# A decode layer on one core: QK in four column groups, one exp per half of K, P permuted by matmuls, PV on 128 columns, shared weights

## Chip, cores, metric

One core of a Trainium2 chip. Its engines are called PE (matmuls), DVE (vector work), ACT (activations, here also copies) and SP (which issues the loads) below; SBUF is the memory that loads land in, PSUM the one that matmuls write to. The metric is the device time of one execution in microseconds (us). The kernel before takes 381.83 us (median of 3 runs, 381.77 to 382.25).

## The reference, cut to what matters

One decode step of a transformer layer: attention over a window of cached keys and values, then a gated MLP, for a batch of 4, one token each.

```python
# B=4, D=576, Hq=32 query heads, Hkv=16, window 4096 of 16384 keys, Dh=128, F=4608, bf16
q = layernorm(x) @ wq                                   # 576 x 4096
k, v = k_cache[:, :, -4096:], v_cache[:, :, -4096:]      # 4 x 16 x 4096 x 128 each
p = softmax(q . k * Dh**-0.5);  o = p . v               # two query heads per kv head
h = x + o @ wo                                          # 4096 x 576
h2 = h + (relu(layernorm(h) @ W_gate) * (layernorm(h) @ W_up)) @ W_down
```

K and V are 67.1 MB each and all the weights 25.4 MB: 159.6 MB have to come in for one input and one output of 4.6 KB each. This is a kernel of loads.

## The kernel before

K and V come in 16 groups each (group `g` is four kv heads of batch `g // 4`, one load of 4.19 MB), into a ring of four slots in SBUF. K's loads run four groups ahead of V's: K4, V0, K5, V1 and so on. One DMA queue issues all loads, in order, and each waits until the last reader of its slot is done. That wait ties the loads to the engines.

```python
def place(name, off, size, reader, make, key=None):       # a load waits for the last reader of its bytes
    for blk in range(off // 64, (off + size) // 64):
        r = owner.get(blk)
        if r is not None and r not in deps: deps.append(r)
        owner[blk] = reader
    P.dma("sync", ("L",) + name, make, semk, deps)
...
place((kind, g), off, TILE, ("QK", g, 1) if kind == "K" else ("PV", g), ...)
```

K has to be turned (DVE transposes 32x32 blocks, in two halves `w` of 128x4096 each), multiplied with q on PE, and after a batch's four groups the softmax follows. PV of group `g - 4` follows QK of group `g` on PE. Its result in PSUM holds more than is wanted, so DVE selects (`select_o`: multiply by a mask, add up).

```python
def pe_qk(g, w, heads=range(4)):
    for a in heads:
        for cb in range(4):
            first = a == cb == 0
            if first:
                deps.append(("TRA", g, w))                # each half of QK waits for its own half of the turn
            ...
            pe(("QK", g, w), lambda e, ...: e.matmul(
                bank[SB[b % 2] + w], lhsT=arena[:, wo_:wo_ + 128],   # 128 columns, mostly zeros (masked q)
                rhs=bass.AP(tensor=arena, offset=off, ap=[[AW, 128], [128, 64]] + steps), ...), deps)

def pe_pv(g):                                             # four column groups of 32, one bank, two banks in turn
    o_ps = bank[OB[g % 2]]
    ...  # PV(g) waits for: L V g, P of this batch, the selection of g - 2
            pe(("PV", g), lambda e, j=j, tq=tq, k=k: e.matmul(
                o_ps[32 * j:32 * j + 32, :], lhsT=pT[:, qd * 1024 + tq * 32:][:, 0:32], rhs=v[:, tq * 512:(tq + 1) * 512], ...), deps)

def do_k(g):                                              # order in the program; each engine runs its part in order
    turn_k(g, 0)
    ...
    flush()                                               # the selection of the PV of the turn before, put off until here
    turn_k(g, 1)
    ...
    pe_qk(g, 0)
    pe_qk(g, 1)
    ...                                                   # then PV(g - 4)
```

## Time and profile before

| | before |
|---|---|
| time, median | 381.83 us |
| span of the profiled run | 379.9 us |
| main load queue | 159.59 MB, 98.0% of 16 engines' span |
| PE / DVE / ACT busy | 74% / 59% / 10% |
| last landing of W_down, then to the end | 376.4 us, 3.5 us |

From the page: busy time of each engine, then the share of the DMA engines and the GB/s in 40 equal slices of the span (a 9 is 90% or more), then the queues with packets, MB and share of 16 engines' span. q1 carries the loads, q8 fetches instructions.

```profile
span 379.9 us, 3671 instructions
...
PE 279.6 (74%) x1629; PEld 93.6 (25%) x1629; DVE 223.1 (59%) x157; ACT 37.6 (10%) x95; POOL 16.5 (4%) x40
...
DMA  8999999999999999999999999999999999999993
GB/s 332 442 414 412 442 442 438 431 400 440 442 440 428 422 421 437 442 431 430 417 435 438 436 417 435 423 438 442 438 412 431 431 436 435 430 433 428 421 405 159
...
q1 hardware_dynamic: 6500, 159.59, 98.0%
q8 instruction: 12, 0.20, 0.2%
```

The DMA row never falls below 9 between its two ends: the loads are the bound. In the packet records a 32 KB packet takes 1.213 us on each of 16 engines, which is 432 GB/s. One batch of K and V (eight loads, 33.6 MB) therefore takes 77.6 us, and a pair of K and V 19.4 us.

The groups that matter, with line, engine, operation, shapes, count, busy time, mean ns of one, and idle time of the engine before them: QK (L453), K's turn (L435) and PV (L500).

```profile
L453 PE MATMUL psb<-sb_arena 128*128 128x512 bf16 x512 | 209.2, 579 | 10.5 <-DVE sb_arena L435 8.0
L435 DVE STREAM_TRANSPOSE sb_arena<-sb_arena 128x4096 f32<-128x4096 f32 x32 | 156.0, 4898 | 47.6 <-DMA sb_arena<-in_A_k_cache_dram 47.6
...
L500 PE MATMUL psb<-sb_arena,sb_pp 128*32 128x512 bf16 x512 | 35.8, 431 | 13.3 <-DMA sb_arena<-in_A_v_cache_dram 6.7
```

From the view of waits (who waited for whom, us in total, times, longest): DVE waits for K's landing, and PE hardly waits for the turn on DVE.

```profile
DVE sb_arena L435 <- DMA sb_arena<-in_A_k_cache_dram: 47.6, 11, 8.4
...
PE psb L453 <- DVE sb_arena L435: 8.0, 3, 3.4
```

And DVE's timeline around one group (start, duration, instruction, and in brackets the idle time before it with what ended it):

```profile
200.64 4.45 DVE L435 STREAM_TRANSPOSE sb_arena<-sb_arena 128x4096 f32<-128x4096 f32 x1 [8.36 <-DMA sb_arena<-in_A_k_cache_dram]
205.01 0.65 DVE L508 TENSOR_TENSOR sb_o_tmp<-psb,sb_qm 128x512 f32<-128x512 f32 x1
205.70 1.04 DVE L512 TENSOR_REDUCE sb_o_sel<-sb_o_tmp 128x128 f32<-128x512 f32 x1
206.66 4.44 DVE L435 STREAM_TRANSPOSE sb_arena<-sb_arena 128x4096 f32<-128x4096 f32 x1
```

### The profile page before, as it was taken

Reading aid. Unit: us, or ns where it says so; the run is one execution under the profiler, and the core shown is the slowest. Engines: PE = TensorE matmul, PEld = TensorE weight load, DVE = VectorE, ACT = ScalarE, POOL = GpSimd, SP = SyncE. Lnnn points to the kernel's source line nnn. Section 1 sums busy time; section 2 is a strip of 40 time slices with the busy share of each in tenths; the row PEclk is TensorE's granted clock in tenths of the full one; section 3 lists DMA queues with packets and bytes.
Section 4 is the critical chain, followed back from the end, with each engine's and each line's share of the span. In section 5 each row is a group of like instructions: output and inputs, shape, how many; then the busy total and the mean of one; then the engine's idle time right before and its main releaser. Section 6 shows DMA issues by size and latency. Waiting matters only on the chain.

```text
span 379.9 us, 3671 instructions
## 1 busy us (share of the span) xinstructions
PE 279.6 (74%) x1629; PEld 93.6 (25%) x1629; DVE 223.1 (59%) x157; ACT 37.6 (10%) x95; POOL 16.5 (4%) x40
## 2 busy tenths in 40 slices
PE   0047999998959992979996939799969537335445
PEld 0022323322222221222222213222212213124224
DVE  0796799979385917875828279756464455012011
ACT  1112000016000007000000050000000340000100
POOL 8800000000000000000000000000000000000000
PEclk9996999999979996798997888989989956756667
DMA  8999999999999999999999999999999999999993
GB/s 332 442 414 412 442 442 438 431 400 440 442 440 428 422 421 437 442 431 430 417 435 438 436 417 435 423 438 442 438 412 431 431 436 435 430 433 428 421 405 159
DMA packets 6522, 159.81 MB, mean 421 GB/s; under 512 B 744, under 2 KB 876, under 8 KB 1516
## 3 DMA queue, kind: packets, MB, share of 16 engines
q1 hardware_dynamic: 6500, 159.59, 98.0%
q8 instruction: 12, 0.20, 0.2%
q14 instruction: 2, 0.02, 0.0%
q10 hardware_dynamic: 8, 0.00, 0.0%
HBM read 159.58 MB, written 0.00 MB: 420 GB/s over the span
## 4 chain that ended last, share of the span: by engine, by line
PE 44%; DMA 37%; DVE 14%; POOL 2%; issue 1%; ACT 0%; SPq 0%; POOLq 0%
PE psb L453 38%; DMA sb_arena<-in_A_k_cache_dram 18%; DMA sb_arena<-in_B_W_down_dram 11%; DVE sb_arena L435 11%; DMA sb_arena<-in_A_v_cache_dram 8%; PE psb L500 4%; POOL sb_arena L303 2%; DVE sb_o_sel L512 1%; DVE sb_o_tmp L508 1%; PE psb L537 0%; ACT sb_arena L421 0%; SPq L286 0%; PE psb L525 0%; PE psb L520 0%; PE psb L472 0%
## 5 line engine op out<-in xcount | busy, mean ns | idle before, releaser
L453 PE MATMUL psb<-sb_arena 128*128 128x512 bf16 x512 | 209.2, 579 | 10.5 <-DVE sb_arena L435 8.0
L435 DVE STREAM_TRANSPOSE sb_arena<-sb_arena 128x4096 f32<-128x4096 f32 x32 | 156.0, 4898 | 47.6 <-DMA sb_arena<-in_A_k_cache_dram 47.6
L453 PEld LDWEIGHTS psb<-sb_arena 128*128 128x128 bf16 x512 | 56.7, 113 | 153.8 <-issue 130.2
L478 ACT ACTIVATE sb_pp<-psb,sb_stat 128x512 bf16<-128x512 f32 x32 | 24.9, 840 | 246.8 <-DVE sb_stat L473 246.8
L500 PE MATMUL psb<-sb_arena,sb_pp 128*32 128x512 bf16 x512 | 35.8, 431 | 13.3 <-DMA sb_arena<-in_A_v_cache_dram 6.7
L500 PEld LDWEIGHTS psb<-sb_arena,sb_pp 128*32 128x32 bf16 x512 | 13.5, 106 | 38.2 <-issue 22.5
L508 DVE TENSOR_TENSOR sb_o_tmp<-psb,sb_qm 128x512 f32<-128x512 f32 x16 | 10.8, 678 | 18.1 <-PE psb L500 18.1
L460 DVE TENSOR_REDUCE sb_stat<-psb 128x1 f32<-128x1024 f32 x4 | 4.8, 1208 | 24.1 <-PE psb L453 24.1
L487 DVE STREAM_TRANSPOSE sb_pp<-sb_pp 128x2048 bf16<-128x2048 bf16 x8 | 18.0, 2277 | 1.4 <-ACT sb_pp L478 1.4
L671 PE MATMUL psb<-sb_arena,sb_hnT 128*32 128x384 bf16 x120 | 9.1, 480 | 11.3 <-DMA sb_arena<-in_B_W_up_dram 8.4
L512 DVE TENSOR_REDUCE sb_o_sel<-sb_o_tmp 128x128 f32<-128x512 f32 x16 | 16.6, 1038 | 0.5
L537 PE MATMUL psb<-sb_o_sel,sb_selw 128*32 128x32 f32 x128 | 2.4, 232 | 16.3 <-DVE sb_o_sel L512 16.3
L678 DVE TENSOR_TENSOR sb_pp<-psb,sb_pp 128x384 bf16<-128x384 f32 x3 | 1.5, 550 | 18.5 <-PE psb L671 18.5
L378 PE MATMUL psb<-sb_ident_b,sb_xn_bf 4*128 4x4 bf16 x4 | 0.3, 174 | 13.7 <-DVE sb_xnd_bf L367 13.7
L391 PE MATMUL psb<-sb_arena,sb_xnT 128*32 128x512 bf16 x32 | 3.6, 631 | 8.9 <-DMA sb_arena<-in_A_wq_dram 8.9
L520 PE MATMUL psb<-sb_stat,sb_sameh 128*128 128x1 f32 x8 | 1.9, 311 | 9.1 <-DVE sb_stat L518 9.1
L671 PEld LDWEIGHTS psb<-sb_arena,sb_hnT 128*32 128x32 bf16 x120 | 4.1, 133 | 15.7 <-DMA sb_arena<-in_B_W_up_dram 8.8
L625 PE MATMUL psb<-sb_arena,sb_oT 128*32 128x288 bf16 x64 | 4.0, 445 | 4.9 <-DMA sb_arena<-in_A_wo_dram 4.9
L303 POOL MEMSET sb_arena<- 128x8192 f32 x1 | 6.9, 6925 | 0.0
L478 ACT ACTIVATION_READ_ACCUMULATOR sb_pp<-psb,sb_stat 128x1 f32 x32 | 6.4, 200 | 0.0
L537 PEld LDWEIGHTS psb<-sb_o_sel,sb_selw 128*32 128x32 f32 x128 | 1.9, 143 | 17.5 <-DVE sb_o_sel L512 17.5
L704 PE MATMUL psb<-sb_arena,sb_pp 128*32 128x144 bf16 x144 | 4.6, 301 | 1.7 <-DMA sb_arena<-in_B_W_down_dram 0.7
(125 smaller groups left out, 73.3 us busy)
## 6 DMA issues: line engine op xcount, KB each, us to landing
sb_arena<-in_A_k_cache_dram SPq DMA_DIRECT2D x16, 4096.0 KB, 17.6
sb_arena<-in_A_v_cache_dram SPq DMA_DIRECT2D x16, 4096.0 KB, 24.3
sb_arena<-in_A_wo_dram SPq DMA_DIRECT2D x1, 4608.0 KB, 26.8
sb_arena<-in_B_W_gate_dram SPq DMA_DIRECT2D x1, 4608.0 KB, 32.0
sb_arena<-in_B_W_up_dram SPq DMA_DIRECT2D x1, 4608.0 KB, 42.2
sb_arena<-in_A_wq_dram SPq DMA_DIRECT2D x1, 4096.0 KB, 21.6
sb_arena<-in_B_W_down_dram SPq DMA_DIRECT2D x3, 1296.0 KB, 40.9
sb_arena<-in_B_W_down_dram SPq DMA_DIRECT2D x1, 864.0 KB, 42.4
```

Of the source, the lines that this page charges most:

```text
L303: pool("c_qW", lambda e: e.memset(arena[:, 0:2 * QWW].bitcast(FP32), 0.0))
L435: dve(("TRA", g, w), lambda e: e.transpose(out=dst, in_=src), [("L", "K", g)] if w == 0 else [])
L453: pe(("QK", g, w), lambda e, off=off, steps=steps, wo_=wo_, qd=qd, first=first, last=a == cb == 3: e.matmul(bank[SB[b % 2] + w], lhsT=aren ...
L460: dve(("MAX", b), lambda e: e.tensor_reduce(out=stat[:, b, 0:1], in_=s_ps, axis=AX.X, op=ALU.max, negate=True), [("QK", 4 * b + 3, 1)])
L478: act(("EXP", b, w), lambda e, w=w, a=a: e.activation(out=bass.AP(tensor=pp, offset=4096 + a // 2 * 2048 + w * 1024 + a % 2, ap=[[8192, 12 ...
L487: dve(("PTR", b, w), lambda e: e.transpose(out=dst, in_=src), [("EXP", b, w), ("PV", 4 * b - 1) if b else "QMM"])
L500: pe(("PV", g), lambda e, j=j, tq=tq, k=k: e.matmul(o_ps[32 * j:32 * j + 32, :], lhsT=pT[:, qd * 1024 + tq * 32:][:, 0:32], rhs=v[:, tq * ...
L508: dve(("OS", g), lambda e: e.tensor_tensor(out=o_tmp[:, :].rearrange("p (t d) -> p t d", t=4), in0=o_ps.rearrange("p (t d) -> p t d", t=4) ...
L512: dve(("OSEL", g), lambda e: e.tensor_reduce(out=o_sel[:, qd, :], in_=o_tmp[:, :].rearrange("p (t d) -> p d t", t=4), axis=AX.X, op=ALU.ad ...
L537: pe(("OT", b), lambda e, q=q, qd=qd: e.matmul(ot_ps[32 * qd:32 * qd + 32, 0:32], lhsT=selw[:, qd, 32 * q:32 * q + 32], rhs=o_sel[:, qd, 3 ...
L671: pe(("GU", g, c // 4), lambda e, g=g, m=m, j=j, lo=lo, c=c: e.matmul(bank[3 * g + m][32 * j:32 * j + 32, 0:384], lhsT=hnT[:, c if c < 4 e ...
L704: pe("DOWN", lambda e, j=j, r=r, n=n, wv=wv: e.matmul(bank[0][32 * n:32 * n + 32, 0:144], lhsT=hhT[:, r * 128 + 32 * j:r * 128 + 32 * j + 32],
```

## The change

Its intent is to take work off PE and ACT. QK no longer multiplies by a 128-column matrix that is mostly zeros; each of four heads has its own group of 32 columns, and the four run side by side. The scores then stand by head, one exp per half does (8 instead of 32). P stands in other rows than V wants, so 64 small matmuls permute it and 32 masked copies spread it. PV now multiplies 128 columns at once into four banks. Matmuls that follow each other with the same weights load them once (`mm_same`). The up-projection weights come in two pieces, and DOWN uses two column groups of 288 instead of four of 144.

```diff
+def mm_same(e, out, lhsT, rhs, start, stop, tile, pos):      # a matmul that keeps the weights of the one before
+    return e.add_instruction(mybir.InstMatmult(... ldweights=False, ...))
...
-        def pe_qk(g, w, heads=range(4)):
+        def pe_qk(g):
+            for cb in range(4):
+                for w in range(2):
+                    for a in range(4):
+                        if cb == w == a == 0:
+                            deps = [("TRA", g, 1)]
+                            if qd == 0 and b:
+                                deps += [("EXP", b - 1, 1), ("MAX", b - 1), ("EV", b - 1, 1)]
+                        lhsT = arena[:, b * 2048 + cb * 512 + g % 4 * 128 + a * 32:][:, 0:32]
+                        out_ = bank[w][32 * a:32 * a + 32, :]
+                        # w == 1: mm_same(...), else e.matmul(...)
...
+        def remap(b):                                        # P to V's rows, then spread under a mask
+            for n in range(4):
+                for i in range(4):
+                    pe(("RM", b, n // 2), ... lhsT=to_v[:, n, :], ...)
+            for h in range(2):
+                for a in range(4):
+                    deps = [("RM", b, h), ("PV", 4 * b - 1) if b else "QMM"] if a == 0 else []
+                    if h: dve(("EV", b, 1), ... e.tensor_scalar(out=out_, in0=src, scalar1=m4[:, a:a + 1], ...), deps)
+                    else: act(("EV", b, 0), ... e.activation(out=out_, in_=src, func=ACT.Copy, scale=m4[:, a:a + 1]), deps)
...
         def pe_pv(g):
-                        deps = [("L", "V", g), ("PTR", b, 0), ("PTR", b, 1), ("OS", g - 2) if g >= 2 else "xT"]
+                        deps = [("L", "V", g), ("EV", b, 0), ("EV", b, 1)] + ([("OSD", g - 1), ("OSC", g - 1)] if g else [])
+                    lhsT = pT[:, qd * 1024 + k * 128:][:, 0:128]
+                    # into bank[2 + j]; j > 0: mm_same(...)
...
         for g in range(NTILE):
+            turn_k(g, 0)
+            if g == 4: soft(0); remap(0)
+            flush()                                          # the selection
+            turn_k(g, 1)
+            pe_qk(g)
+            if g % 4 == 3 and g > 3: soft(g // 4)
+            if g >= 4: do_v(g - 4)
+            if g % 4 == 3 and g > 3: remap(g // 4)
```

Because the two halves of QK share weights, `w` moved inside the loop over `cb`, and QK now waits for the second half of the turn.

## The prediction

> **What bounds the kernel now: the load queue.** The page's queue line gives 159.59 MB on the main queue, 98.0% of 16 engines' span; the slice row for DMA reads 9 from slice 2 to 39. In the trace's packet records a 32 KB packet takes 1.213 us on each of 16 engines, 432 GB/s, nearly everywhere. The Trainium skill ("DMA: Bandwidth & Descriptors", Specifications) gives a fabric ceiling of 435 GB/s; this trace agrees. 159.6 MB at 432 GB/s is 369 us. The rest of the 379.9 us span: loads start moving at 2.2 to 3.0 us; most engines finish at 373, but three only at 376.05; last landing 376.4; then 3.5 us of tail (last W_down matmuls, copy, store). The late engines: twelve 16 KB instruction fetches share these engines, and each delays its engine by about 1.5 us; an engine with two is 3 us late, and the last landing waits for the latest.
>
> PE (74% busy), DVE (59%), ACT (10%) are not the bound. The chain of waits shows "PE 44%", but through slot releases, while the queue is practically never empty.
>
> **What the change does.**
> - Bytes loaded: unchanged. Order: wq before the first K; the up-projection weights in two pieces.
> - QK: 512 matmuls of 128 columns at 441 ns become 512 in four column groups. Estimate 3.5 us per K group instead of 14.1, if four strided streams run side by side as PV's four contiguous ones did (1.84 us per 32).
> - PV: from 1.84 us per group to 32 full-width matmuls; estimate 4 x 1.84 = 7.4 us (twice that at a 0.5 clock).
> - Sum per group 11 us instead of 16, against 19.4 us of loading per K+V pair. PE busy falls from 280 to about 200 us.
> - Softmax: 32 exps (840 ns each) become 8; P's transposes shrink from 18 us to about 5; new are 64 small permutation matmuls and 32 masked copies (0.4 to 0.6 us each). V's selection costs DVE about 1 us more per group. The slow K transposes (first pair 14.3 us against 8.9) go, saving 13 us. DVE about 215 us, ACT about 40.
> - 768 of 1454 matmuls load no weights: about 9 instruction fetches instead of 12.
> - The tail: up's last part leaves 1 us of gate/up work after landing instead of 4. DOWN uses two column groups of 288 instead of four of 144, so up to twice as slow (240 ns per step at clock 0.5), but starts about 3 us earlier.
>
> **On the critical path:** almost nothing. The queue keeps its bytes and rate; slots come free sooner (before, the load issued at 41.1 us came as the queue ran dry near 43 us, costing about 0.4 us; that goes). Fewer fetches take perhaps 0 to 1.5 us off the last landing, by chance of where they fall. The tail may change by a few tenths.
>
> **Predicted: 380.8 us, 379.0 to 382.6 us.** Chances: faster by over 2% 0.02, within 2% 0.95, slower 0.03.
>
> **Signs of being right:** DMA still 97 to 98% of the span; last W_down landing 374.5 to 376.5 us; PE busy near 200 us, idle before PV; ACT and DVE little changed; longer queue waits for slots that never empty the queue.
>
> **What would make it wrong:** strided streams not running side by side, or a PE clock mostly at 0.5, so that QK+PV pass 19.4 us per pair and starve the queue (slower); a gap in the loads where the new softmax chain holds up PV 12 to 15, and with it wo's load; DOWN falling behind the last landing (1 to 3 us slower); or a load rate above 432 GB/s, which nothing here suggests.

## More of the kernel before

DVE waited 8.36 us for K to land, turned its first half, made the selection of the last PV (L508, L512), and turned the second half. The chain of waits has PE starting QK of the first half at 205.14 us, while DVE is still selecting: PE and DVE overlap here.

## The result, and the profile after

403.07 us (median of 4, 402.58 to 405.1) against 382.04 us for the kernel before. A ratio here is the mean time of one kernel's fast runs over that of the other's of the same rounds, so not quite the ratio of the medians: 1.056, 95% interval 1.053 to 1.060. The change is slower, by well over the range that was predicted.

| | before | after |
|---|---|---|
| span | 379.9 us | 403.2 us |
| PE / DVE / ACT busy | 279.6 / 223.1 / 37.6 us | 216.4 / 228.0 / 54.2 us |
| main queue, share of the span | 98.0% | 93.0% |
| one batch of loads, V6's issue to V10's | 77.8 us | 86.3 us |
| last landing of W_down | 376.4 us | 394.7 us |
| from it to the end | 3.5 us | 8.5 us |
| end of the last PV | 332.0 us | 371.1 us |

("One batch" is the time between the issue of V's loads 6 and 10 on the load queue: 167.14 and 244.89 us before, 181.00 and 267.34 us after.) The profiled run after was the slowest of its four (405.1 us), so these figures are 2 us on the high side of the median. Of the 23.3 us between the spans, 18.3 are a later last landing and 5.0 a longer end. In the packet records each DMA engine is idle for 17.6 us on average between its first packet and the last few microseconds, against 0.9 us before. That is nearly all of the later landing.

The page after:

```profile
span 403.2 us, 2703 instructions
...
PE 216.4 (54%) x1495; PEld 40.9 (10%) x727; DVE 228.0 (57%) x202; ACT 54.2 (13%) x89; POOL 16.2 (4%) x39
...
DMA  9999999999999999769999999399999997999990
GB/s 361 419 416 462 418 419 452 429 419 434 440 423 423 452 421 419 325 260 416 410 427 424 436 423 436 128 419 413 423 423 436 434 429 328 395 417 411 418 403 10
...
q1 hardware_dynamic: 6632, 159.59, 93.0%
q8 instruction: 9, 0.15, 0.1%
```

The same 159.59 MB come in, but the GB/s row has holes: 325 and 260, 128, and 328 near the end. Two stretches of the span, with busy time and instructions of each engine, granted clock, DMA share and GB/s, show the first hole:

```profile
160.00:170.00 10.00, 0.06 (x4) 0.06 (x4) 9.92 (x7) 0.00 (x0) 0.00 (x0) 0.52 0.88 380
170.00:180.00 10.00, 10.00 (x61) 1.36 (x24) 4.26 (x2) 0.00 (x0) 0.00 (x0) 0.80 0.53 210
```

From 160 to 170 us PE did nothing and DVE was busy throughout; from 170 to 180 us PE was busy throughout and DVE less than half. Neither is the bound over the whole, yet each waits for the other. The load queue in that stretch (the start of an issue):

```profile
173.90 0.53 SPq L247 DMA_DIRECT2D sb_arena<-in_A_k_cache_dram  x1
181.00 0.54 SPq L247 DMA_DIRECT2D sb_arena<-in_A_v_cache_dram  x1
```

The load issued at 173.90 us waited for QK to finish with its slot, and the queue had nothing else to do: from 169.90 to 174.20 us the view of windows shows a DMA share of 0.00.

The groups: the turn, QK (L466 with L34 for the matmuls that share weights) and PV (L530 with L34).

```profile
L442 DVE STREAM_TRANSPOSE sb_arena<-sb_arena 128x4096 f32<-128x4096 f32 x32 | 141.0, 4430 | 12.2 <-DMA sb_arena<-in_A_k_cache_dram 12.2
L466 PE MATMUL psb<-sb_arena 128*32 128x512 bf16 x256 | 42.2, 628 | 137.4 <-DVE sb_arena L442 137.4
L34 PE MATMUL psb<-sb_arena,sb_pp 128*128 128x512 bf16 x384 | 108.9, 394 | 0.0
L530 PE MATMUL psb<-sb_arena,sb_pp 128*128 128x512 bf16 x128 | 50.9, 398 | 9.3 <-DVE sb_o_tmp L543 9.3
...
L34 PE MATMUL psb<-sb_arena 128*32 128x512 bf16 x256 | 44.1, 652 | 0.0
```

QK's four strided streams do run side by side: 32 matmuls take 3.9 us, PV's 32 take 7.0 us. The estimates were 3.5 and 7.4. The waits:

```profile
PE psb L466 <- DVE sb_arena L442: 137.4, 16, 14.6
...
DVE sb_arena L442 <- DMA sb_arena<-in_A_k_cache_dram: 12.2, 8, 2.4
```

PE now waits 137 us for K's turn, where it waited 8. And DVE waits 12 us for K to land instead of 48: K is there, DVE is late. (L34 is the line of the helper `mm_same`, so QK and PV share it and are told apart by shapes.) DVE's timeline around one ordinary group:

```profile
201.26 1.38 DVE L543 TENSOR_TENSOR sb_o_tmp<-psb,sb_fm 32x512 f32<-32x512 f32 x2 [7.00 <-PE psb L34]
202.67 0.69 DVE L546 TENSOR_TENSOR sb_o_tmp<-sb_o_tmp,sb_fm 64x512 f32<-64x512 f32 x1
203.39 1.02 DVE L547 TENSOR_REDUCE sb_o_sel<-sb_o_tmp 128x128 f32<-128x512 f32 x1
204.33 8.76 DVE L442 STREAM_TRANSPOSE sb_arena<-sb_arena 128x4096 f32<-128x4096 f32 x2
219.66 1.38 DVE L543 TENSOR_TENSOR sb_o_tmp<-psb,sb_fm 32x512 f32<-32x512 f32 x2 [6.57 <-PE psb L34]
```

From one selection (201.26) to the next (219.66) are 18.4 us, and they are a ring: selection 3.1 us, second half of the next K's turn 4.4 us, QK 3.9 us (to 212.65, by the load queue's issue), PV 7.0 us, selection. Each waits for the one before. DVE sits idle for 6.57 us of it, PE for 7.5. And at the end of a batch:

```profile
146.73 1.38 DVE L491 STREAM_TRANSPOSE sb_pp<-sb_pp 128x512 bf16<-128x512 bf16 x2 [0.84 <-ACT sb_pp L487]
155.42 2.73 DVE L508 TENSOR_SCALAR sb_pp<-psb,sb_m 128x512 bf16<-128x512 f32 x4 [7.31 <-PE psb L497]
158.07 4.43 DVE L442 STREAM_TRANSPOSE sb_arena<-sb_arena 128x4096 f32<-128x4096 f32 x1
162.43 1.34 DVE L543 TENSOR_TENSOR sb_o_tmp<-psb,sb_fm 32x512 f32<-32x512 f32 x2
...
165.45 8.76 DVE L442 STREAM_TRANSPOSE sb_arena<-sb_arena 128x4096 f32<-128x4096 f32 x2
```

DVE waits 7.31 us for the permutation, which stands behind a PV on PE, before it makes its half of the masked copies (L508). The next K's turn stands behind those copies in DVE's order, and its second half behind another selection: it is done at 169.9 us, about 23 us after the softmax's transposes of P began (146.73).

### The profile page after: what moved, and what is told of

It reads as the page before. It is cut to its first block, busy times and chain, and to the rows that moved or that the text cites. A ratio compares the mean times of both kernels' runs of the same rounds, so it can differ in the third digit from the quotient of the medians.

```text
span 403.2 us, 2703 instructions
## 1 busy us (share of the span) xinstructions
PE 216.4 (54%) x1495; PEld 40.9 (10%) x727; DVE 228.0 (57%) x202; ACT 54.2 (13%) x89; POOL 16.2 (4%) x39
## 3 DMA queue, kind: packets, MB, share of 16 engines
q1 hardware_dynamic: 6632, 159.59, 93.0%
## 4 chain that ended last, share of the span: by engine, by line
PE 50%; DVE 36%; DMA 12%; issue 1%; ACT 0%; SPq 0%; DVEq 0%
PE psb L34 29%; DVE sb_arena L442 18%; DMA sb_arena<-in_A_k_cache_dram 12%; PE psb L530 8%; PE psb L466 6%; DVE sb_o_tmp L543 5%; DVE sb_o_sel L547 3%; DVE sb_pp L508 3%; DVE sb_o_tmp L546 2%; DVE sb_stat L471 1%; PE psb L726 1%; PE psb L497 1%; PE psb L646 1%; PE psb L688 1%; PE psb L638 0%
## 5 line engine op out<-in xcount | busy, mean ns | idle before, releaser
L442 DVE STREAM_TRANSPOSE sb_arena<-sb_arena 128x4096 f32<-128x4096 f32 x32 | 141.0, 4430 | 12.2 <-DMA sb_arena<-in_A_k_cache_dram 12.2
L466 PE MATMUL psb<-sb_arena 128*32 128x512 bf16 x256 | 42.2, 628 | 137.4 <-DVE sb_arena L442 137.4
L34 PE MATMUL psb<-sb_arena,sb_pp 128*128 128x512 bf16 x384 | 108.9, 394 | 0.0
L530 PE MATMUL psb<-sb_arena,sb_pp 128*128 128x512 bf16 x128 | 50.9, 398 | 9.3 <-DVE sb_o_tmp L543 9.3
L543 DVE TENSOR_TENSOR sb_o_tmp<-psb,sb_fm 32x512 f32<-32x512 f32 x32 | 21.7, 678 | 55.0 <-PE psb L34 54.7
L540 ACT COPY sb_o_tmp<-psb 32x512 f32<-32x512 f32 x32 | 18.5, 578 | 204.5 <-PE psb L34 204.2
L34 PE MATMUL psb<-sb_arena 128*32 128x512 bf16 x256 | 44.1, 652 | 0.0
L466 PEld LDWEIGHTS psb<-sb_arena 128*32 128x32 bf16 x256 | 9.7, 120 | 179.6 <-DVE sb_arena L442 150.6
L530 PEld LDWEIGHTS psb<-sb_arena,sb_pp 128*128 128x128 bf16 x128 | 12.9, 101 | 113.6 <-issue 113.6
L508 DVE TENSOR_SCALAR sb_pp<-psb,sb_m 128x512 bf16<-128x512 f32 x16 | 10.9, 744 | 21.5 <-PE psb L497 21.5
L487 ACT ACTIVATE sb_pp<-psb,sb_stat 128x512 bf16<-128x512 f32 x8 | 5.4, 683 | 80.7 <-DVE sb_stat L483 80.7
L546 DVE TENSOR_TENSOR sb_o_tmp<-sb_o_tmp,sb_fm 64x512 f32<-64x512 f32 x16 | 11.0, 689 | 0.5
L34 PE MATMUL psb<-sb_arena,sb_hnT 128*32 128x384 bf16 x80 | 6.0, 383 | 0.0
## 6 DMA issues: line engine op xcount, KB each, us to landing
sb_arena<-in_A_wq_dram SPq DMA_DIRECT2D x1, 4096.0 KB, 12.2
```

Of the source, the lines that this page charges most:

```text
L34: return e.add_instruction(mybir.InstMatmult(name=e.bass.get_next_instruction_name(), engine=mybir.EngineType.PE, ins=[e.lower_ap(rhs), e. ...
L442: dve(("TRA", g, w), lambda e: e.transpose(out=dst, in_=src), [("L", "K", g)] if w == 0 else [])
L466: fn = lambda e, out_=out_, lhsT=lhsT, rhs=rhs, start=start, stop=stop: e.matmul(out_, lhsT=lhsT, rhs=rhs, start=start, stop=stop, skip_gr ...
L508: dve(("EV", b, 1), lambda e, out_=out_, src=src, a=a: e.tensor_scalar(out=out_, in0=src, scalar1=m4[:, a:a + 1], scalar2=None, op0=ALU.mu ...
L530: fn = lambda e, lhsT=lhsT, rhs=rhs, k=k, j=j: e.matmul(bank[2 + j], lhsT=lhsT, rhs=rhs, start=(k == 0), stop=(k == 7), skip_group_check=True)
L540: act(("OSC", g), lambda e, j=j: e.copy(out=o_tmp[32 * j:32 * j + 32, 0:512], in_=bank[2 + j][32 * j:32 * j + 32, :]), [("PV", g), ("OSEL" ...
```

## The experiments

Theory A: the changed kernel is bound by a ring of waits through DVE and PE, because QK waits for both halves of the turn and a selection stands between the halves. 18.4 us per group leave 1 us against 19.4 us of loading, and the longer end of a batch cannot be made up: 86 us per batch against 77.6. Rival B: PE's own work, at its granted clock of 0.79 (the share of full speed that the profile shows), is too much. Rival C: only the chain at a batch's end empties the queue.

### 1. The selection later in DVE's order

```diff
-            flush()
             turn_k(g, 1)
             pe_qk(g)
+            flush()
```

> The changed kernel with the selection of O moved from between the two halves of K's turn to after QK in program order; all engines do the same work. Theory A (a ring of waits through DVE and PE: selection 3.1 us, second half of the turn 4.4, QK 3.9, PV 7.0, so 18.4 us per group, plus about 31 us where a batch ends, makes 86 us per batch against 77.6 us of loading): the ring opens, the queue is nearly never empty, 382 to 388 us. Rival B (PE's own work at a clock of 0.79 is too much): unchanged, 401 to 405. Rival C (only the chain at a batch's end empties the queue): little, 396 to 403.

Measured: 380.75 us (380.26 to 381.81), ratio to the kernel before 0.9975 (0.9956 to 0.9993). PE's and DVE's busy times stay (217.1 and 229.4 us). A batch takes 77.7 us, the rate of the loads; the last landing is at 374.8 us.

```profile
span 378.1 us, 2703 instructions
...
PE 217.1 (57%) x1495; PEld 40.8 (11%) x727; DVE 229.4 (61%) x202; ACT 54.1 (14%) x89; POOL 16.1 (4%) x39
...
DMA  8999999999999999999999999999999999999994
GB/s 333 444 437 430 416 435 444 437 416 426 438 438 433 419 430 438 433 433 419 433 439 426 426 433 437 432 430 426 430 440 430 428 433 430 432 429 414 421 428 203
...
q1 hardware_dynamic: 6632, 159.59, 98.4%
```

```profile
PE psb L466 <- DVE sb_arena L442: 99.5, 13, 13.0
...
DVE sb_arena L442 <- DMA sb_arena<-in_A_k_cache_dram: 38.7, 14, 7.3
```

```profile
200.29 8.77 DVE L442 STREAM_TRANSPOSE sb_arena<-sb_arena 128x4096 f32<-128x4096 f32 x2 [7.33 <-DMA sb_arena<-in_A_k_cache_dram]
209.10 1.38 DVE L543 TENSOR_TENSOR sb_o_tmp<-psb,sb_fm 32x512 f32<-32x512 f32 x2
...
211.23 1.14 DVE L547 TENSOR_REDUCE sb_o_sel<-sb_o_tmp 128x128 f32<-128x512 f32 x1
```

The DMA row has no hole. DVE turns both halves in one go as soon as K lands, for which it waits (7.33 us), and selects afterwards, while PE works on QK. This takes back 22.3 us (403.07 to 380.75), all of the loss and a little more, with the same work in another order (PE busy 217.1 us, at a granted clock of 0.84), so rival B falls. V's issues from V6 to V10 are 17.4, 15.0, 21.9 and 23.5 us apart: the end of a batch still takes longer than 19.4 us, but the groups before it leave room, so rival C alone does not explain the loss either. PV's new wait for the selection of the PV before it (it now has one set of banks instead of two) is still in this kernel, so that wait alone does not empty the queue. PE still waits 99.5 us for the turn, but now because K has not landed: the same line in the waits view is harmless here and was the cost before. What tells them apart is the line for DVE, which waits 38.7 us for the load instead of 12.2.

### 2. The masked copies on ACT

```diff
-                    if h:
-                        dve(("EV", b, 1), ... e.tensor_scalar(...), deps)
-                    else:
-                        act(("EV", b, 0), ...)
+                    act(("EV", b, h), ...)
```

> The changed kernel with DVE's half of the masked copies of P done by ACT, so DVE does not wait for the permutation behind PV and can turn the next K. Theory A: only the end of a batch gets shorter, by 2 to 6 us in each of three, so 388 to 398 us. Rival C (the chain at a batch's end alone): 382 to 387. Rival B: unchanged, 401 to 405.

Measured: 400.13 us (397.26 to 403.12), ratio 1.048. A batch takes 83.3 us, 3 less. The mechanism has the expected size per batch, but the total lies just above the 388 to 398 us that theory A expected: the last landing comes 6.7 us earlier in the profile (388.0 us), but the end after it takes 10.4 us instead of 8.5. Rival C falls in the form tested, with DVE's copies as the chain. The rest of that chain is still there: V9's issue to V10's takes 23.7 us, 26.5 before this edit. Experiment 1 has 23.5 us at the same place and keeps the queue full; the difference is in the other three intervals, which are 18.6 to 21.2 us here with the ring closed and 15.0 to 21.9 us there.

### 3. QK half by half

`w` outermost in QK again, each half waiting for its own half of the turn, column groups kept, each matmul loading its weights.

```diff
-            for cb in range(4):
-                for w in range(2):
+            for w in range(2):
+                for cb in range(4):
                     for a in range(4):
-                        if cb == w == a == 0:
-                            deps = [("TRA", g, 1)]
+                        if cb == a == 0:
+                            deps = [("TRA", g, w)]
```

> The changed kernel with QK's column groups kept, but the two halves of K one after the other, each waiting for its own half of the turn, and each matmul loading its weights (sharing them is what makes QK wait for both halves). Theory A: about 2 us per group out of the ring, 8 per batch, so per batch about 78.5 against 77.6 us of loading: 384 to 392 us. Rivals B and C: 400 to 405.

Measured: 384.42 us (382.27 to 386.04), ratio 1.006; a batch takes 79.0 us, where 78.5 was expected. Taking 2 us per group out of the ring, with more weight loads on PE, brings back most of the loss. What remains fits the 1.4 us by which a batch still exceeds the loads.

### 4. PV in four column groups

Only rows `32j` to `32j + 31` of bank `2 + j` are ever read, so PV needs only 32 columns for each.

```diff
-                        fn = ... mm_same(e, bank[2 + j], lhsT, rhs, ..., (128, 128), (0, 0))
+                        fn = ... e.matmul(bank[2 + j][32 * j:32 * j + 32, :], lhsT=lhsT[:, 32 * j:32 * j + 32], rhs=rhs, ...)
```

> The changed kernel with PV again on 32 columns in four column groups (only the rows of its own column group are ever read of each bank, so the result stays right): PV 1.9 us instead of 7.0 per group. Theory A and rival B both: 5 us per group less, 20 per batch, the queue is not emptied, 380 to 386 us; and the end after V's last load shortens, as PV 12 to 15 no longer follow each other at 8.6 us. Rival C: the end of a batch still holds the queue up, 390 to 400.

Measured: 382.01 us (381.42 to 382.59), ratio 1.000; a batch takes 78.2 us. PE busy falls to 141.1 us. With 5 us per group out of the ring, the end of a batch no longer matters. A PV stands in the chain at a batch's end too, so taken alone this tells theory A from neither rival; the first experiment did.

### 5. No shared weights

`mm_same` replaced by an ordinary matmul, same order, so QK still waits for both halves.

> The changed kernel with every matmul loading its own weights again, in the same order, QK still waiting for both halves of the turn. Theory A (the ring of waits): sharing is no part of the ring but through that wait, so unchanged, 400 to 406 us, PE busy about the same, 12 instruction fetches instead of 9. A rival by which the matmuls without a weight load are themselves what costs: 380 to 390.

Measured: 404.06 us (402.0 to 407.3), ratio 1.059, with 12 instruction fetches instead of 9; a batch takes 88.0 us. Sharing weights costs and gains nothing measurable here. (This profile's batch is 1.7 us longer than that of the changed kernel, though its run was shorter, 402.0 against 405.1 us: a batch's time from one profile is no surer than that.) Its harm is the order it asked for.

### 6. The ring, put into the kernel before

```diff
-                        deps.append(("TRA", g, w))
+                        deps.append(("TRA", g, 1))
```

> The kernel before, changed in one word: QK of the first half of K waits for both halves of the turn, as the changed kernel's does. Theory A: the same ring closes here, per group selection 1.7, second half of the turn 4.5, QK 14.1, PV 1.8, so 22 us, and a longer end of a batch, 95 to 105 us per batch against 77.6 us of loading: 425 to 455 us with no other work added. If the wait for both halves is not what closes the ring: 381 to 388.

Measured: 434.62 us (434.03 to 435.38), ratio 1.138; a batch takes 97.3 us.

```profile
GB/s 340 436 436 432 412 430 424 432 339 248 291 432 419 357 436 338 424 70 436 292 345 430 339 435 342 433 53 436 291 379 397 347 430 339 435 434 436 431 395 220
...
q1 hardware_dynamic: 6500, 159.59, 87.1%
```

```profile
PE psb L453 <- DVE sb_arena L435: 72.5, 15, 9.8
...
DVE sb_arena L435 <- DMA sb_arena<-in_A_k_cache_dram: 31.0, 8, 6.6
```

With no work added (PE busy 276.8 us, 279.6 before), the one wait costs 53 us. PE's wait for the turn goes from 8.0 to 72.5 us. The load queue shows the period of the ring (the start of each issue):

```profile
218.56 0.53 SPq L247 DMA_DIRECT2D sb_arena<-in_A_v_cache_dram  x1
240.58 0.53 SPq L247 DMA_DIRECT2D sb_arena<-in_A_v_cache_dram  x1
262.60 0.53 SPq L247 DMA_DIRECT2D sb_arena<-in_A_v_cache_dram  x1
```

Two ordinary groups take 22.02 us each, and the sum around the ring is 22 us. So the one wait is enough to close a ring of the expected period: the kernel before was safe not because its sum of PE work was small, but because QK's first half kept PE busy while DVE selected.

### 7. Selection later, no shared weights

> The first experiment (selection later) with every matmul loading its own weights: the ring is open, the loads bind, and 12 instruction fetches instead of 9 share the DMA engines, about 1.5 us of one engine each. Expected 380.5 to 382.5 us: no time for the weight loads themselves, 0 to 1.6 us from the last landing, by which engines the fetches hit.

Measured: 382.52 us (381.25 to 382.61), ratio 1.001, just outside what was expected; last landing at 376.1 us instead of 374.8. The page lists 11 fetches within the span where 12 were expected, and 9 in experiment 1. It fits the idea that a fetch delays the engine it falls on, but one profile each does not prove it.

### 8. Selection later, PV twice

PV's loop run twice, the second pass starting the sums anew.

> The first experiment with PV done twice over (the second pass starts the sums anew, so the result stays right): PE's sum per group is 3.9 + 14 = 17.8 us, still under the 19.4 us of loading. Theory A: with the ring open the sum alone counts, so the queue stays full while K and V are loaded, 78 to 82 us per batch; but PV 12 to 15, 15.3 us apart, then finish about 25 us later and the chain after them ends the kernel: 398 to 412 us. Rival B (PE's work at its clock bound the changed kernel): the queue runs empty in every batch, over 420.

Measured: 449.84 us (448.66 to 451.0), ratio 1.178; a batch takes 92.3 us. The expectation missed: the queue does run empty, and the total lies where rival B put it (over 420 us), not in theory A's 398 to 412. PE is busy for only 74% of the span, so its work alone does not fill the time. Its intervals between V's issues from V6 to V10 are 23.8, 17.8, 20.4 and 30.3 us. The 17.8 is PE's sum, as expected with the ring open. But the other three add 21 us around a batch's end, which theory A had taken as nearly free once the selection was moved. Rival C holds a part of the truth: the chain at a batch's end is a cost of its own, hidden only where the other groups leave room.

### 9. PV twice, masked copies on ACT

> PV done twice (449.8 us, 92.2 us per batch where 78 to 82 were expected) with DVE's half of the masked copies moved to ACT as well. The miss is put down to the end of a batch: where PE's sum is 17.8 us per group the intervals there were 20, 30 and 24, as the next K's turn stands behind the copies on DVE, which wait for the permutation behind PV. If so, moving the copies lets the turn run during PV: 6 to 10 us per batch less, 82 to 86 us, and 420 to 435 us in all. If PE's work itself is what takes 92 us: 447 to 452.

Measured: 438.01 us (434.88 to 438.94), ratio 1.148; a batch takes 84.0 us, within the expectation. The total lies between the two ranges (420 to 435 if the chain is the cause, 447 to 452 if PE's work is): the end after the last landing takes 20.5 us, 19.2 in experiment 8, and keeps part of what the batches gained. So the copies before the next K's turn were about 8 of those 21 us per batch; the rest (softmax, weights of the selection, half-clock stretches) was not taken apart.

### 10. Selection later, masked copies on ACT, PV once

> Selection later and the copies on ACT together, PV once: both cures of the changed kernel. The loads bind already with the first alone (380.75 us), so no further gain: 379.5 to 381.5 us, with the queue never empty and a last landing at 374 to 376 us.

Measured: 381.09 us (380.8 to 381.8, 5 rounds), ratio 0.998 (0.9965 to 0.999). No more than the first experiment alone: the loads bind, and nothing on the engines can buy more. Experiments 1 and 10 are the best versions, faster than the kernel before by about 0.25%, which lies just clear of the intervals but far under 2%.

| | us | us per batch | PE busy us |
|---|---|---|---|
| before | 381.83 | 77.8 | 279.6 |
| after | 403.07 | 86.3 | 216.4 |
| 1 selection later | 380.75 | 77.7 | 217.1 |
| 2 copies on ACT | 400.13 | 83.3 | 218.9 |
| 3 QK by halves | 384.42 | 79.0 | 220.5 |
| 4 PV in column groups | 382.01 | 78.2 | 141.1 |
| 5 no shared weights | 404.06 | 88.0 | 213.1 |
| 6 before, waits for both halves | 434.62 | 97.3 | 276.8 |
| 7 selection later, no shared weights | 382.52 | 77.9 | 218.9 |
| 8 selection later, PV twice | 449.84 | 92.3 | 329.2 |
| 9 PV twice, copies on ACT | 438.01 | 84.0 | 328.2 |
| 10 selection later, copies on ACT | 381.09 | 77.8 | 218.8 |

PE busy time does not order the times. The time per batch does, to within 0.3 us of it, but for experiments 8 and 9, where PV twice also lengthens the end after the last landing (19.2 and 20.5 us, where the others take 3 to 10).

## Why the prediction was wrong

- **The bound of the kernel before: right.** 432 GB/s against the 435 GB/s of the Trainium skill ("DMA: Bandwidth & Descriptors", Specifications). Experiment 1 has 62 us less of PE's work than the kernel before (217.1 against 279.6) and gains 1 us.
- **The sizes: mostly right.** QK 3.9 us per group (3.5 said), PV 7.0 (7.4), PE busy 216 us (200), DVE 228 (215), 9 fetches (9). ACT was underestimated, 54 us instead of 40: its copies for the selection (18.5 us, a group of its own in the profile) were left out.
- **The step that failed:** "Sum per group 11 us instead of 16, against 19.4 us of loading per K+V pair", and from it that "slots come free sooner" and "longer queue waits for slots that never empty the queue". The sum of one engine's work bounds the rate only if the engines overlap. In the new order they do not: the period of a group is selection + half a turn + QK + PV = 18.4 us, through two engines that each take their instructions in order. The Trainium skill says so of DVE and ACT ("TensorE: Matmul & The Clock Gate", Architectural detail: strict FIFO), and that matmuls stay in program order (the same page, Step-by-step). This trace agrees for DVE: it sits idle for 7.00 us before the selection at 201.26 us, although the second half of K, which needs nothing but the landing that the first half has had, is ready; that turn starts only behind the selection, at 204.33 us. The diff showed the wait for `("TRA", g, 1)`, and it was not followed around. The queue did empty (93.0% of the span instead of the 97 to 98% forecast), and PE waited 137.4 us for the turn.
- **The end of a batch was left out of the sum.** 26.5 us there (V9's issue to V10's) and 21.2 in the softmax's group bring a batch to 86.3 us: the ring of 18.4 us alone is just under the 19.4 us of loading, and it is ring and batch end together that exceed it. The prediction named this danger, for PV 12 to 15 only, and gave slower a chance of 0.03.
- **"The tail may change by a few tenths": wrong, 5.0 us.** PV 12 to 15 start 11.8, 9.9 and 8.6 us apart, as each waits for the selection of the one before from the same banks; the last ends at 371.1 us, 28 us after V's last landing (4 us before). WO, the norm and the MLP then end the kernel without waiting for W_down: DOWN ran 4.6 us in one piece. In experiment 1 the same chain starts at 343.2 us and stays hidden.
- **The bound itself was predicted well for a kernel whose ring is open:** experiment 1 has the last landing at 374.8 us (374.5 to 376.5 said) and 380.75 us (380.8 said), closer than the runs agree among themselves (380.26 to 381.81).

## What to carry to other kernels

When a change takes work off an engine that is not the bound, do not compare sums of work with the bound; walk once around every loop of waits (which instruction stands before which on each in-order engine, and what does it wait for) and compare the longest loop's period with it. Sharing weights between two halves of a stream asks for both halves at once, and can close such a loop. Slack work such as a selection belongs behind the work that the other engine waits for.

## What the Trainium skill lacked or had wrong

- "DMA: Bandwidth & Descriptors", Specifications, lists about 358 GB/s as the limit of HBM per core; this core, alone, loaded at 432 GB/s. The same page, Bandwidth, has 425 GB/s for a single core with the pair's other core idle, which agrees (what the other core did here is not on record); the table alone misleads.
- "TensorE: Matmul & The Clock Gate" has no figure for a moving operand that steps over elements. Another page, "SBUF — State Buffer", has a rule for how far one can step, but no time for a matmul. In the kernel before, it depended on the pattern: in five halves of QK, which step evenly by two elements, 512 columns took 216 ns from start to start at the full granted clock and 427 ns at half; in the others, which read pairs four elements apart with 16 from pair to pair, they took 431 ns at the full clock and 430 ns at half (16 in 7.06 us), so that there the clock made no difference. Contiguous ones with kept weights took 216 ns. Four streams of the second pattern in column groups still ran side by side, 32 in 3.9 us.
- "TensorE: Matmul & The Clock Gate", Back-to-back issue gap, gives a sustained 131 ns per matmul of 512 columns. PV's full-width matmuls ran at 216 ns each at the full granted clock, one weight load for four, and so did the evenly stepped ones of QK in the kernel before, with a weight load each; 216 ns is the page's figure for an isolated matmul.
- No page says what an instruction fetch costs the loads. "Runtime: NRT & Kernel Launch", Instruction fetch mechanics, has blocks of 16 KiB; the packet records here show such a block (about 1.07 us) in the middle of a stream of data packets, the next data packet about 0.5 us longer, on one of the 16 engines. This is so for at least 9 of the 12 fetches before; of the 9 after, some fell where the queue was idle.
- No page tells how to judge a ring of waits through two in-order engines by its period; the waits view names the two engines, and only the timeline shows the 18.4 us.
